# Random-feature attention and a feed-forward layer on one core: the exact fp32 projections done per head on 64 rows of the array

## The chip, the core and the metric

The kernel runs on one core of one Trainium2 chip. The metric is the device time of one execution in microseconds (us), taken as the median of several runs.

The core has five engines with queues of their own that run in order: TensorE (PE, matmuls into PSUM), VectorE (DVE), ScalarE (ACT), GpSimd (POOL) and SyncE (SP, which issues nearly all DMAs). They wait for each other by semaphores. PSUM has eight banks of 128 partitions x 512 fp32 values.

## The reference

```python
def _attn_ref(q, k, v, omega):              # q, k, v: (8, 8, 576, 64) fp32; omega: (128, 64)
    scale = 1.0 / np.sqrt(np.sqrt(D))
    q_s, k_s = (q * scale, k * scale)
    def phi(x):
        proj = np.einsum('bhsd,md->bhsm', x, omega)
        h = proj - np.sum(x * x, axis=-1, keepdims=True) / 2.0
        h = h - np.max(h, axis=-1, keepdims=True)
        return np.exp(h) / np.sqrt(m)
    q_p, k_p = (phi(q_s), phi(k_s))
    kv = np.einsum('bhsm,bhsd->bhmd', k_p, v)
    z = np.sum(k_p, axis=2)
    num = np.einsum('bhsm,bhmd->bhsd', q_p, kv)
    den = np.einsum('bhsm,bhm->bhs', q_p, z)[..., None] + 1e-06
    return num / den

def _moe_ref(x, w_in, w_out):               # x: (4608, 512) from the heads; w_in 512x2048, w_out 2048x512
    h = x @ w_in
    g = h - np.tanh(h)
    return g @ w_out
```

The term with the sum of squares is the same for all features of a token and falls out against the row maximum, so the kernel computes exp(proj - max proj) alone.

## The kernel before

Heads are taken two at a time: a pair `c` (four of them) has 128 rows of `qT` or `kT`, 64 of one head and 64 of the other, and tokens along the free dimension. A *k unit* (`k_unit(b, c)`) makes the features of the 576 keys of one batch and pair and sums them with the values into `pk`. A *q unit* (`q_unit(ch, c)`) makes the features of 256 queries (a chunk `ch`), divides them by the denominator (`L351`, `L354`, `L358`, `L360`), transposes them (`L367`) and multiplies with the k sums (`L375`). Both are generators: `tick` advances every one that is open by one piece, so that pieces of several units stand in turns in the program. A scheduler then places each engine's instructions, and the order on each engine is fixed when the program is built.

Two arithmetics are in use. The *native* one (fp32 matmuls) serves the k units of batches 0 and 1 and the q units of chunks 0, 1 and 2: 8 k units and 12 q units, all in the first stage of the program. The rest split fp32 values in two parts and use a faster format. This text is about the native ones, in `features_f`. There the stationary operand of a matmul is a block of 128 tokens of `f` (all 128 rows, both heads), and the moving one is `om_bd`, 128 rows x 256 columns: the scaled omega of head 0 in rows 0 to 63 and columns 0 to 127, that of head 1 in the other corner, and zeros elsewhere (`L105` to `L108`, made by POOL). One matmul so gives the features of both heads for 128 tokens, 256 columns. A call takes two token blocks: 512 columns, one PSUM bank `pj`. DVE takes the four row minima in one instruction (`L162`), and ACT makes four exponentials (`L164`). A k unit makes two such calls, and one more matmul for the last 64 tokens (`L198`, with `oms`, the scaled omega with no zeros beside it). A q unit makes one call. The `pj` banks go round among four (`pj0`, `pj1`, `po0`, `po1`), then three from step 16 on.

In the same stage the 16 blocks of weights (`raw`, 1 MB each, loaded by SP in one queue with `qf`, `kf` and `v`) are decoded: ACT `L439` and `L441`, POOL `L442`, DVE `L444`, `L445` and `L448`, ACT `L452`, DVE `L453` and `L454`. The buffer `m` of a decode exists once. The first feed-forward products (`L471`) stand at the end of that stage, and from there on the feed-forward layer runs with the other units between its pieces.

Of the kernel before, what the change touches and what calls it, by code (L numbers as in the profile page):

```python
# [8 lines left out]
F32 = mybir.dt.float32  # L9
# [22 lines left out]
def favor_attention_ffn(ctx: ExitStack, tc: tile.TileContext, qT, kT, va, vb, vt, omT, w, out):  # L32
# [11 lines left out]
    nc = tc.nc  # L44
# [4 lines left out]
    sb = ctx.enter_context(tc.tile_pool(name="sb", bufs=1))  # L49
    ps = ctx.enter_context(tc.tile_pool(name="ps", bufs=1, space=bass.MemoryType.PSUM))  # L50
# [34 lines left out]
    ident = const.tile([P, P], F32, name="ident")  # L85
    junk = const.tile([P, M], F32, name="junk")
# [7 lines left out]
    a0 = open_pool("a0")  # L94
    omf = a0.tile([P, M], F32, name="omf")
# [6 lines left out]
    nc.scalar.activation(ones, ident, AF.Copy, bias=1.0, scale=0.0)  # L102
    om2 = om.rearrange("p a m -> p (a m)")

    om_bd = a0.tile([P, 2, M], F32, name="om_bd")  # L105
    nc.gpsimd.memset(om_bd, 0.0)
    nc.gpsimd.tensor_scalar(om_bd[0:D, 0], omf[0:D], -SCALE, 1.0, op0=ALU.mult, op1=ALU.mult)
    nc.gpsimd.tensor_scalar(om_bd[D:P, 1], omf[D:P], -SCALE, 1.0, op0=ALU.mult, op1=ALU.mult)  # L108

    oms = a0.tile([P, M], F32, name="oms")  # L110
    nc.gpsimd.tensor_scalar(oms, omf, -SCALE, 1.0, op0=ALU.mult, op1=ALU.mult)

    def kv_tiles(pool, names):

# [17 lines left out]
    def features(lhs, name):  # L132

        n = len(lhs)
        ph = att("phi", [P, 4, M], F32, f"phi_{name}")
        nb = sb.tile([P, 4], F32, tag="nb", name=f"nb_{name}", bufs=12)

        for g in range(0, n, 2):
            m = min(2, n - g)
            pj = ps.tile([P, 2, 2 * M], F32, tag=bank("pj"), name=f"pj_{name}_{g}")  # L140
            for i in range(m):
                nc.tensor.matmul(pj[:, i], lhs[g + i], om2, start=True, stop=True)  # L142
            nc.scalar.copy(ph[:, g : g + m], pj[:, :m, M:])  # L143
            for i in range(m):
                j = g + i
                nc.vector.tensor_tensor_reduce(  # L146
                    ph[:, j], pj[:, i, :M], ph[:, j], scale=-SCALE, scalar=3.0e38,
                    op0=ALU.add, op1=ALU.min, accum_out=nb[:, j : j + 1])
        for j in range(n):
            nc.scalar.activation(ph[:, j], ph[:, j], AF.Exp, bias=nb[:, j : j + 1], scale=-1.0)  # L150
        return ph

    def features_f(f, toks, name):

        n = 2 * len(toks)
        ph = att("phi", [P, 4, M], F32, f"phi_{name}")
        nb = sb.tile([P, 4], F32, tag="nb", name=f"nb_{name}", bufs=12)
        pj = ps.tile([P, 4, M], F32, tag=bank("pj"), name=f"pj_{name}")
        for i, (a, b) in enumerate(toks):
            nc.tensor.matmul(pj[:, 2 * i : 2 * i + 2].rearrange("p a m -> p (a m)"), f[:, a:b],  # L160
                             om_bd.rearrange("p a m -> p (a m)"), start=True, stop=True)
        nc.vector.tensor_reduce(nb[:, :n], pj[:, :n], axis=AX.X, op=ALU.min)  # L162
        for j in range(n):
            nc.scalar.activation(ph[:, j], pj[:, j], AF.Exp, bias=nb[:, j : j + 1], scale=-1.0)  # L164
        return ph

    kvf = {}
    kvs = {}

    def k_unit(b, c):  # L170

        n = f"{b}_{c}"
        if not mode["native"]:
            f = att("kf", [P, S], F32, f"kf_{n}")
# [3 lines left out]
        f = att("kf", [P, 4 * P], F32, f"kf_{n}")  # L178
# [1 line left out]
        if (b, c) == (0, 0):  # L180
            fetch(0)
        v, kd = bank("v"), bank("kd")
        halves = [slice(0, D), slice(D, P)]
# [4 lines left out]
        for h, r in enumerate(halves):  # L188
            load(v[r, 4 + h, 0:D], vb[b, c, r])
        yield  # L190
        phs = []
        for t in range(0, 4, 2):
            phs.append(features_f(f, [(t * P, t * P + P), (t * P + P, t * P + 2 * P)], f"k{t}_{n}"))
            yield
        ph = att("ph5", [P, M], F32, f"ph5_{n}")
        nb = sb.tile([P, 4], F32, tag="nb", name=f"nb5_{n}", bufs=12)
        pj = ps.tile([P, M], F32, tag=bank("pj"), name=f"pj5_{n}")
        nc.tensor.matmul(pj, kd, oms, start=True, stop=True)  # L198
        nc.vector.tensor_reduce(nb[:, 0:1], pj, axis=AX.X, op=ALU.min)
# [2 lines left out]
        pk = ps.tile([P, 512], F32, tag=bank("pk"), name=f"pk_{n}")  # L202
        nc.tensor.matmul(pk[:, 0 : 2 * E], ph, v[:, 4:6].rearrange("p h e -> p (h e)"),
                         start=True, stop=False)
        for h in range(2):
            for t in range(4):
                nc.tensor.matmul(pk[:, E * h : E * h + E], phs[t // 2][:, 2 * (t % 2) + h],
                                 v[:, 6 * h + t], start=False, stop=(h, t) == (1, 3))
            if h == 0:
                yield  # L210
# [109 lines left out]
    def q_unit(ch, c):  # L320

        n = f"{ch}_{c}"
        t0 = ch * TC
        pieces = []
        t = t0
        while t < t0 + TC:
            e = min((t // S + 1) * S, t0 + TC)
            pieces.append((t // S, t - t0, e - t0))
            t = e
        f = att("qf", [P, TC], F32, f"qf_{n}")  # L330
# [1 line left out]
        load(f, qT[c, :, t0 : t0 + TC])  # L332
        yield
        if native:
            ph = features_f(f, [(0, P), (P, 2 * P)], f"q{n}")
            ix = lambda h, t: 2 * t + h
        else:
            x = att("qx", [P, 2, TC], F32R, f"qx_{n}")
            split_rows(x, f)
            yield  # L340
            ph = features([x[:, h, t * P : (t + 1) * P] for h in range(2) for t in range(2)], f"q{n}")
            ix = lambda h, t: 2 * h + t
        dn = sb.tile([P, 4], F32, tag="dn", name=f"dn_{n}", bufs=8)
# [24 lines left out]
        if native:
            qf = att("qt", [P, 2, TC], F32, f"qt_{n}")
            nc.scalar.copy(qf.rearrange("p h t -> p (h t)"), pt)  # L370
# [144 lines left out]
    def tick(new=(), force=False):  # L515
# [13 lines left out]
        pt=["pt", "h1"], h=["h0", "h1"])  # L529
# [5 lines left out]
    start = {}  # L535
# [54 lines left out]
    start = {}  # L590
# [76 lines left out]
```

## Time and profile before

| what | value |
|---|---|
| median of 3 runs | 1079.37 us (1078.85 to 1082.38) |
| profiled execution | 1079.19 us, its span 1077.4 us |
| PE busy over the span | 1048.9 us (97%) |
| DVE, ACT, POOL busy | 851.9 us (79%), 714.4 us (66%), 317.1 us (29%) |
| L160, the native projections: PE records | 64 for the k units, 48 for the q units |

The span is the time from the first to the last instruction of the profiled execution; the metric counts 1.8 us more around it. The chain of work that ended last lies on PE nearly throughout, in the feed-forward products. One fp32 matmul of the program shows as two records on PE and as two weight loads (PEld). In a timeline row the first number is the start, the second the time from the start to the end of the instructions of the row, and `x8` their number; a bracket gives the idle time ahead of it on its engine and what ended it.

### The profile page before, as it was taken

What the parts mean: (1) busy time and instruction counts of PE and PEld (TensorE: products, weight loads), DVE (VectorE), ACT (ScalarE), POOL (GpSimd) and SP (SyncE); (2) the same over time, 40 slices, a digit from 0 to 9 for tenths busy, and PEclk for the clock granted to TensorE, in tenths of its full rate; (3) what the DMA queues carried; (4) which work ended last, traced back from release to release, by engine and by line L of the source; (5) the groups of instructions that cost most, each with busy time, mean ns of one, the idle gap of its engine ahead of it and who ended that gap; (6) DMA issues with size and microseconds to landing.
All of it is one profiled execution on the core that took longest, in us unless ns stands there. A gap on an engine that the chain in (4) does not pass through costs nothing. (4 is left out here: it accounts for less than half of the span.)

```text
span 1077.4 us, 20348 instructions
## 1 busy us (share of the span) xinstructions
PE 1048.9 (97%) x6760; PEld 954.1 (89%) x6760; DVE 851.9 (79%) x3028; ACT 714.4 (66%) x1833; POOL 317.1 (29%) x526
## 2 busy tenths in 40 slices
PE   6889999998999999999999999999999999999998
PEld 5777788997999999999999998999999999999997
DVE  6899695798898886688888888898888887666522
ACT  5898564767777675677776766777767775556422
POOL 6333350344433330033333333233333331000000
PEclk8899999998999999999999999999999999999999
DMA  7653300211111110011111111021111110000000
GB/s 249 175 192 130 149 1 17 71 33 52 33 52 33 43 43 20 21 52 33 42 38 33 53 33 50 15 62 33 42 32 48 34 41 11 30 11 26 1 21 20
DMA packets 37194, 55.91 MB, mean 52 GB/s; under 512 B 13921, under 2 KB 23265, under 8 KB 35041
## 3 DMA queue, kind: packets, MB, share of 16 engines
q1 hardware_dynamic: 37008, 54.57, 16.1%
q8 instruction: 54, 0.88, 0.3%
q14 instruction: 52, 0.42, 0.1%
q10 hardware_dynamic: 80, 0.03, 0.0%
HBM read 45.15 MB, written 9.44 MB: 51 GB/s over the span
## 5 line engine op out<-in xcount | busy, mean ns | idle before, releaser
L471 PE MATMUL h<-xh,w 128*128 128x256 f32 (+1 forms) x2176 | 454.0, 292 | 3.1 <-DVE g L476 2.7
L471 PEld LDWEIGHTS h<-xh,w 128*128 128x128 f32 x2176 | 357.0, 191 | 13.3 <-DVE g L476 3.4
L471 PE MATMUL h<-xl,w 128*128 128x256 f32 (+1 forms) x1088 | 317.0, 291 | 0.5 <-DVE xl L411 0.5
L489 PE MATMUL po<-w,gh 128*128 128x512 f32 x544 | 214.3, 394 | 0.0
L471 PEld LDWEIGHTS h<-xl,w 128*128 128x128 f32 x1088 | 207.9, 191 | 6.7 <-DVE xl L411 0.8
L490 PE MATMUL po<-w,gh 128*128 128x512 f32 x544 | 213.7, 393 | 0.0
L491 PE MATMUL po<-w,gl 128*128 128x512 f32 x544 | 209.9, 391 | 0.0
L476 DVE TENSOR_TENSOR g<-h,g 128x512 f32<-128x512 f32 x144 | 98.9, 687 | 65.8 <-ACT g L475 64.9
L475 ACT ACTIVATE g<-h 128x512 f32<-128x512 f32 x144 | 85.2, 591 | 97.8 <-PE h L471 91.2
L477 ACT CAST gh<-g 128x512 fp32r<-128x512 f32 x144 | 89.4, 621 | 88.3 <-DVE g L476 85.3
L478 DVE TENSOR_TENSOR gl<-g,gh 128x512 fp32r<-128x512 f32 x144 | 111.2, 772 | 43.2 <-ACT gh L477 35.9
L491 PEld LDWEIGHTS po<-w,gl 128*128 128x128 f32 x544 | 102.2, 188 | 20.6
L489 PEld LDWEIGHTS po<-w,gh 128*128 128x128 f32 x544 | 102.6, 189 | 16.6 <-ACT gh L477 0.2
L490 PEld LDWEIGHTS po<-w,gh 128*128 128x128 f32 x544 | 102.5, 188 | 15.1
L351 DVE CUSTOM_DVE_ANT_0 junk<-phi_q,zb 128x128 f32<-128x128 f32 (+1 forms) x320 | 96.5, 304 | 15.0 <-ACT phi_q L150 0.8
L442 POOL TENSOR_SCALAR a<-a 128x1024 f32<-128x1024 f32 x16 | 63.7, 3986 | 88.0 <-ACT a L439 85.1
L254 POOL TENSOR_TENSOR khl<-phi_ka,khl 128x256 fp32r<-128x256 f32 x48 | 37.6, 785 | 159.7 <-DVE khl L253 142.3
L150 ACT ACTIVATE phi_q<-phi_q,nb_q 128x128 f32<-128x128 f32 x240 | 79.1, 392 | 4.7 <-DVE nb_q L146 4.3
L262 POOL CAST vhl<-v 128x128 fp32r<-128x128 f32 (+1 forms) x144 | 45.2, 315 | 99.5 <-PE pk L270 80.2
L391 DVE TENSOR_TENSOR ql<-pt,qh 128x512 fp32r<-128x512 f32 x60 | 41.1, 685 | 26.5 <-ACT qh L390 26.2
L146 DVE CUSTOM_DVE_ANT_0 phi_q<-pj_q,phi_q 128x128 f32<-128x128 f32 x240 | 55.8, 284 | 2.8 <-ACT phi_q L143 2.5
L263 DVE TENSOR_TENSOR vhl<-v,vhl 128x128 fp32r<-128x128 f32 (+1 forms) x144 | 44.3, 308 | 16.9 <-POOL vhl L262 13.2
(148 smaller groups left out, 1949.8 us busy)
## 6 DMA issues: line engine op xcount, KB each, us to landing
raw<-w SPq DMA_DIRECT2D x16, 1024.0 KB, 6.3
qf<-qT SPq DMA_DIRECT2D x72, 128.0 KB, 2.1
out<-o SPq DMA_DIRECT2D x36, 256.0 KB, 2.0
kf<-kT SPq DMA_DIRECT2D x24, 288.0 KB, 2.9
v<-vt SPq DMA_DIRECT2D x24, 288.0 KB, 2.9
kf<-kT SPq DMA_DIRECT2D x8, 256.0 KB, 4.1
v<-va SPq DMA_DIRECT2D x16, 128.0 KB, 3.4
kd<-kT SPq DMA_DIRECT2D x16, 16.0 KB, 4.1
```

What stands on the lines that cost most here:

```text
L146: nc.vector.tensor_tensor_reduce(ph[:, j], pj[:, i, :M], ph[:, j], scale=-SCALE, scalar=3.0e38, op0=ALU.add, op1=ALU.min, accum_out=nb[:, ...
L150: nc.scalar.activation(ph[:, j], ph[:, j], AF.Exp, bias=nb[:, j : j + 1], scale=-1.0)
L351: nc.vector.tensor_tensor_reduce(bank("junk")[r], ph[r, i], kvs[b, c][1][r, h], scale=1.0, scalar=EPS, op0=ALU.mult, op1=ALU.add, accum_ou ...
L442: nc.gpsimd.tensor_scalar(a.bitcast(F32), a.bitcast(F32), 2.0**-15, 122879.9921875, op0=ALU.max, op1=ALU.min)
L471: nc.tensor.matmul(o, w_, x, start=i == 0, stop=i == len(prods) - 1)
L475: nc.scalar.activation(g, p, AF.Tanh)
L476: nc.vector.tensor_sub(g, p, g)
L477: nc.scalar.copy(gh, g)
L478: nc.vector.tensor_sub(gl, g, gh.bitcast(F32))
L489: nc.tensor.matmul(po[t], h, wt[f][:, 0, DM:], start=first, stop=False)
L490: nc.tensor.matmul(po[t], h, wt[f][:, 1, DM:], start=False, stop=False)
L491: nc.tensor.matmul(po[t], l, wt[f][:, 0, DM:], start=False, stop=last)
```

## The change

Each head of a pair is now projected by itself. The moving operand is `oms`, 64 rows x 128 columns, and the stationary one is the 64 rows of that head; the built program puts each matmul on one half of the array's rows (rows 0 to 63, or 64 to 127). The two heads are written in turns and go to two different banks, `pjs[0]` and `pjs[1]`. `om_bd` is gone. A k unit makes one call for its four token blocks: eight matmuls of 128 columns in place of four of 256, two minima of 512 columns and eight exponentials as before, on two banks as before. A q unit makes four matmuls of 128 columns in place of two of 256, and it now uses two banks and two minima of 256 columns, in place of one bank and one of 512. The columns of `phi` and of `dn` stand head by head.

```diff
-    om_bd = a0.tile([P, 2, M], F32, name="om_bd")
-    nc.gpsimd.memset(om_bd, 0.0)
-    nc.gpsimd.tensor_scalar(om_bd[0:D, 0], omf[0:D], -SCALE, 1.0, op0=ALU.mult, op1=ALU.mult)
-    nc.gpsimd.tensor_scalar(om_bd[D:P, 1], omf[D:P], -SCALE, 1.0, op0=ALU.mult, op1=ALU.mult)
-
     oms = a0.tile([P, M], F32, name="oms")
     nc.gpsimd.tensor_scalar(oms, omf, -SCALE, 1.0, op0=ALU.mult, op1=ALU.mult)
+
+    halves = [slice(0, D), slice(D, P)]
...
-    def features_f(f, toks, name):
-
-        n = 2 * len(toks)
-        ph = att("phi", [P, 4, M], F32, f"phi_{name}")
-        nb = sb.tile([P, 4], F32, tag="nb", name=f"nb_{name}", bufs=12)
-        pj = ps.tile([P, 4, M], F32, tag=bank("pj"), name=f"pj_{name}")
-        for i, (a, b) in enumerate(toks):
-            nc.tensor.matmul(pj[:, 2 * i : 2 * i + 2].rearrange("p a m -> p (a m)"), f[:, a:b],
-                             om_bd.rearrange("p a m -> p (a m)"), start=True, stop=True)
-        nc.vector.tensor_reduce(nb[:, :n], pj[:, :n], axis=AX.X, op=ALU.min)
-        for j in range(n):
-            nc.scalar.activation(ph[:, j], pj[:, j], AF.Exp, bias=nb[:, j : j + 1], scale=-1.0)
-        return ph
+    def features_f(f, n, name):
+
+
+        if n == 2:
+            ph = att("phi", [P, 4, M], F32, f"phi_{name}")
+            phs = [ph[:, 0:2], ph[:, 2:4]]
+        else:
+            phs = [att("phi", [P, 4, M], F32, f"phi_{name}_{h}") for h in range(2)]
+        nb = sb.tile([P, 8], F32, tag="nb", name=f"nb_{name}", bufs=12)
+        pjs = [ps.tile([P, 4, M], F32, tag=bank("pj"), name=f"pj_{name}_{h}") for h in range(2)]
+        for t in range(n):
+            for h, r in enumerate(halves):
+                nc.tensor.matmul(pjs[h][:, t], f[r, t * P : (t + 1) * P], oms[r], start=True, stop=True)
+        for h in range(2):
+            b = nb[:, 4 * h : 4 * h + n]
+            nc.vector.tensor_reduce(b, pjs[h][:, :n], axis=AX.X, op=ALU.min)
+            for t in range(n):
+                nc.scalar.activation(phs[h][:, t], pjs[h][:, t], AF.Exp, bias=b[:, t : t + 1], scale=-1.0)
+        return phs
...
-        phs = []
-        for t in range(0, 4, 2):
-            phs.append(features_f(f, [(t * P, t * P + P), (t * P + P, t * P + 2 * P)], f"k{t}_{n}"))
-            yield
+        phs = features_f(f, 4, f"k{n}")
+        yield
+        yield
...
-                nc.tensor.matmul(pk[:, E * h : E * h + E], phs[t // 2][:, 2 * (t % 2) + h],
+                nc.tensor.matmul(pk[:, E * h : E * h + E], phs[h][:, t],
                                  v[:, 6 * h + t], start=False, stop=(h, t) == (1, 3))
...
-            ph = features_f(f, [(0, P), (P, 2 * P)], f"q{n}")
-            ix = lambda h, t: 2 * t + h
+            ph = features_f(f, 2, f"q{n}")
+            at = lambda h, t: ph[h][:, t]
```

The scheduler places the instructions of the first stage anew. On every engine the order is the same, row for row, from the last native q unit on (on PE from its products `pn_3`, `L375`, at 113.68 us in the profile); SP's order is the same throughout. Three places of the first stage are shown. Lines of the changed kernel stand one lower than before from `L198` on, and `L162`, `L165` and `L167` are now the projections, the minima and the exponentials.

**PE**, from the end of the second k unit over the third k unit and the first q unit to the sums `pk` of the second (the names of k units end in batch, pair and buffer number before, and in pair, head and buffer number now; pairs count from 0). Before:

```order
L160 MATMUL pj_k_0_1_218<-om_bd,kf_1_186 128x256 x2
L198 MATMUL pj_0_1_258<-oms,kd_126 128x128
L225 MATMUL pk_0_210<-ident,z_0_252 128x128 x2
L160 MATMUL pj_k_0_2_264<-om_bd,kf_2_226 128x256 x2
L160 MATMUL pj_k_0_2_286<-om_bd,kf_2_226 128x256 x2
L160 MATMUL pj_q_0_296<-om_bd,qf_0_272 128x256 x2
L203 MATMUL pk_1_278<-v_123,ph_0_1_256 128x132
L207 MATMUL pk_1_278<-v_123,phi_k_0_1_200 128x66 x2
```

Now:

```order
L162 MATMUL pj_k_1_0_202<-oms,kf_1_185 128x128
L162 MATMUL pj_k_1_1_203<-oms,kf_1_185 128x128
L199 MATMUL pj_0_1_260<-oms,kd_122 128x128
L226 MATMUL pk_0_222<-ident,z_0_254 128x128 x2
L162 MATMUL pj_k_2_0_267<-oms,kf_2_228 128x128 x4
L162 MATMUL pj_k_2_1_268<-oms,kf_2_228 128x128 x4
L162 MATMUL pj_q_0_0_301<-oms,qf_0_287 128x128 x2
L204 MATMUL pk_1_293<-v_119,ph_0_1_258 128x132
L208 MATMUL pk_1_293<-v_119,phi_k_1_0_199 128x66 x4
L162 MATMUL pj_q_0_1_302<-oms,qf_0_287 128x128 x2
L208 MATMUL pk_1_293<-v_119,phi_k_1_1_200 128x66 x4
```

The alternation of the heads as written stands in PE's queue for the first two k units alone (the first two rows end the second of them). From the third on, the four blocks of head 0 stand together, and then the four of head 1. The projection of a q unit is in two pieces, and here the second of them stands behind half of the sums `pk`.

**ACT**, from its first exponentials on (`a` and `m` are the buffers of a decode, `w` its result). Before:

```order
L164 ACTIVATE phi_k_0_0_152<-pj_k_0_0_154,nb_k_0_0_153 128x128 x4
L439 ACTIVATE a_162<-raw_142 128x1024
L441 ACTIVATE m_163<-raw_142 128x1024
L164 ACTIVATE phi_k_0_0_176<-pj_k_0_0_178,nb_k_0_0_177 128x128 x4
L200 ACTIVATE ph_0_0_194<-pj_0_0_196,nb_0_0_195 128x128
L439 ACTIVATE a_234<-raw_150 128x1024
L452 CAST w_170<-a_162 128x1024
L222 COPY kvf_106<-pk_0_210 128x64 x2
L441 ACTIVATE m_235<-raw_150 128x1024
L439 ACTIVATE a_357<-raw_174 128x1024
```

Now:

```order
L440 ACTIVATE a_171<-raw_138 128x1024
L442 ACTIVATE m_172<-raw_138 128x1024
L167 ACTIVATE phi_k_0_0_148<-pj_k_0_0_151,nb_k_0_150 128x128 x4
L167 ACTIVATE phi_k_0_1_149<-pj_k_0_1_152,nb_k_0_150 128x128 x4
L201 ACTIVATE ph_0_0_193<-pj_0_0_195,nb_0_0_194 128x128
L440 ACTIVATE a_236<-raw_146 128x1024
L453 CAST w_179<-a_171 128x1024
L223 COPY kvf_102<-pk_0_222 128x64 x2
L442 ACTIVATE m_237<-raw_146 128x1024
L440 ACTIVATE a_379<-raw_183 128x1024
```

The first two instructions of the first decode have moved ahead of the first eight exponentials.

**DVE**, around the minima of the third k unit and of the first q unit. Before:

```order
L162 TENSOR_REDUCE nb_k_0_2_285<-pj_k_0_2_286 128x4
L454 SCALAR_TENSOR_TENSOR w_242<-m_235,a_234 128x1024
L444 TENSOR_SCALAR a_357<-a_357 128x1024
L162 TENSOR_REDUCE nb_q_0_295<-pj_q_0_296 128x4
L445 SCALAR_TENSOR_TENSOR a_357<-raw_174,a_357 128x1024
L214 COPY z_1_326<-pk_1_278 128x2
L448 SCALAR_TENSOR_TENSOR m_358<-raw_174,m_358 128x1024
L199 TENSOR_REDUCE nb_0_2_331<-pj_0_2_332 128x1
L162 TENSOR_REDUCE nb_k_0_3_344<-pj_k_0_3_345 128x4
L351 ISA junk,dn_0_304<-phi_q_0_294,zb_0_276 128x128
```

Now:

```order
L445 TENSOR_SCALAR a_379<-a_379 128x1024
L446 SCALAR_TENSOR_TENSOR a_379<-raw_183,a_379 128x1024
L165 TENSOR_REDUCE nb_k_2_266<-pj_k_2_1_268 128x4
L165 TENSOR_REDUCE nb_q_0_300<-pj_q_0_0_301 128x2
L449 SCALAR_TENSOR_TENSOR m_380<-raw_183,m_380 128x1024
L352 ISA junk,dn_0_313<-phi_q_0_299,zb_0_291 128x128
L352 ISA dn_0_313 128x1
L352 ISA junk_101,dn_0_313<-phi_q_0_299,zb_0_291 128x128
L352 ISA dn_0_313 128x1
L165 TENSOR_REDUCE nb_q_0_300<-pj_q_0_1_302 128x2
```

`z_1`, which waits for the sums `pk` of the second k unit, stood right behind this piece of the third decode; it has moved further down, behind the denominators (`L352`, shown as ISA) and the end of that decode. The minima of the q unit are two, with other work between them.

More of the change, by code (lines that the diff above doesn't have):

```diff
@@ L151, in features @@
         return ph
-    def features_f(f, toks, name):
-        n = 2 * len(toks)
-        ph = att("phi", [P, 4, M], F32, f"phi_{name}")
-        nb = sb.tile([P, 4], F32, tag="nb", name=f"nb_{name}", bufs=12)
-        pj = ps.tile([P, 4, M], F32, tag=bank("pj"), name=f"pj_{name}")
-        for i, (a, b) in enumerate(toks):
-            nc.tensor.matmul(pj[:, 2 * i : 2 * i + 2].rearrange("p a m -> p (a m)"), f[:, a:b],
-                             om_bd.rearrange("p a m -> p (a m)"), start=True, stop=True)
-        nc.vector.tensor_reduce(nb[:, :n], pj[:, :n], axis=AX.X, op=ALU.min)
-        for j in range(n):
-            nc.scalar.activation(ph[:, j], pj[:, j], AF.Exp, bias=nb[:, j : j + 1], scale=-1.0)
-        return ph
+    def features_f(f, n, name):
[4 more added lines that the diff above has]
+            phs = [att("phi", [P, 4, M], F32, f"phi_{name}_{h}") for h in range(2)]
+        nb = sb.tile([P, 8], F32, tag="nb", name=f"nb_{name}", bufs=12)
+        pjs = [ps.tile([P, 4, M], F32, tag=bank("pj"), name=f"pj_{name}_{h}") for h in range(2)]
[8 more added lines that the diff above has]
+        return phs
     kvf = {}
@@ L182, in k_unit @@
         v, kd = bank("v"), bank("kd")
-        halves = [slice(0, D), slice(D, P)]
         for r in halves:
@@ L190, in k_unit @@
         yield
-        phs = []
-        for t in range(0, 4, 2):
-            phs.append(features_f(f, [(t * P, t * P + P), (t * P + P, t * P + 2 * P)], f"k{t}_{n}"))
-            yield
+        phs = features_f(f, 4, f"k{n}")
+        yield
+        yield
         ph = att("ph5", [P, M], F32, f"ph5_{n}")
-        nb = sb.tile([P, 4], F32, tag="nb", name=f"nb5_{n}", bufs=12)
+        nb = sb.tile([P, 8], F32, tag="nb", name=f"nb5_{n}", bufs=12)
         pj = ps.tile([P, M], F32, tag=bank("pj"), name=f"pj5_{n}")
@@ L341, in q_unit @@
             ph = features([x[:, h, t * P : (t + 1) * P] for h in range(2) for t in range(2)], f"q{n}")
-            ix = lambda h, t: 2 * h + t
+            at = lambda h, t: ph[:, 2 * h + t]
         dn = sb.tile([P, 4], F32, tag="dn", name=f"dn_{n}", bufs=8)
@@ L345, in q_unit @@
             for t in range(2):
-                i = ix(h, t)
+                i = 2 * h + t
                 for b, s, e in pieces:
@@ L351, in q_unit @@
                         nc.vector.tensor_tensor_reduce(
-                            bank("junk")[r], ph[r, i], kvs[b, c][1][r, h], scale=1.0, scalar=EPS,
+                            bank("junk")[r], at(h, t)[r], kvs[b, c][1][r, h], scale=1.0, scalar=EPS,
                             op0=ALU.mult, op1=ALU.add, accum_out=dn[r, i : i + 1])
@@ L355, in q_unit @@
         for i in range(4):
-            e = bank("norm")
+            e, x = bank("norm"), at(i // 2, i % 2)
             if e is nc.scalar:
-                e.mul(ph[:, i], ph[:, i], dn[:, i : i + 1])
+                e.mul(x, x, dn[:, i : i + 1])
             else:
-                e.tensor_scalar(ph[:, i], ph[:, i], dn[:, i : i + 1], 1.0, op0=ALU.mult, op1=ALU.mult)
+                e.tensor_scalar(x, x, dn[:, i : i + 1], 1.0, op0=ALU.mult, op1=ALU.mult)
         yield
@@ L366, in q_unit @@
         for i in range(4):
-            nc.tensor.transpose(pt[:, i * P : (i + 1) * P], ph[:, ix(i // 2, i % 2)], ident)
+            nc.tensor.transpose(pt[:, i * P : (i + 1) * P], at(i // 2, i % 2), ident)
         if native:
```

## The prediction

> **What bounds the kernel now.** First the page's busy times, then the windows view, which splits the span into stretches (busy time and number of records of PE, PEld, DVE, ACT and POOL, then the granted clock, the DMA share and GB/s).
>
> ```profile
> PE 1048.9 (97%) x6760; PEld 954.1 (89%) x6760; DVE 851.9 (79%) x3028; ACT 714.4 (66%) x1833; POOL 317.1 (29%) x526
> ...
> 0.00:20.00 20.00, 14.74 (x53) 12.82 (x54) 9.25 (x13) 8.61 (x18) 12.55 (x32) 0.76 0.77 246
> 20.00:40.00 20.00, 15.48 (x75) 13.46 (x73) 17.03 (x33) 15.51 (x42) 8.28 (x2) 0.81 0.69 203
> 40.00:110.00 70.00, 59.98 (x340) 50.35 (x341) 68.92 (x216) 63.20 (x172) 23.42 (x6) 1.00 0.45 159
> ...
> 114.00:200.00 86.00, 85.70 (x421) 72.47 (x420) 60.28 (x112) 49.36 (x81) 27.19 (x13) 1.00 0.18 66
> ```
>
> PE is the bound over the whole span, but not where the change is. From 40 to 110 us DVE is busy 68.9 of 70 us, while PE has 10.0 us idle; from 114 us PE has 0.3 us idle in 86. So the native stage is DVE's until about 110 us, and what comes behind it is PE's. Where the two meet is read from the timeline:
>
> ```profile
> 97.42 0.50 PE L471 MATMUL h<-xh,w 128*128 128x512 f32 x1 [1.60 <-DVE g L476]
> 109.55 0.50 PE L471 MATMUL h<-xh,w 128*128 128x512 f32 x1 [0.78 <-DVE g L476]
> ...
> 113.68 1.36 PE L375 MATMUL pn<-qt,kvf 128*128 128x64 f32 x8 [0.68 <-ACT qt L370]
> ```
>
> Twice the feed-forward products wait for a DVE subtraction that stands in DVE's full queue; from 113.68 us on the order of all engines is unchanged. My reading is therefore that the change counts by what it does to DVE's queue up to about 110 us, and that a shift there goes through to the end one for one. What PE gains or loses in projections counts only beyond its 10.0 us of idle time.
>
> **The projections on PE.** Starts in a row without idle time give what one matmul costs:
>
> ```profile
> 70.01 1.03 PE L160 MATMUL pj_q<-om_bd,qf 128*128 128x256 f32 x4
> 70.88 0.38 PE L225 MATMUL pk<-ident,z 128*128 128x128 f32 x2
> 71.09 1.03 PE L160 MATMUL pj_q<-om_bd,qf 128*128 128x256 f32 x4
> ...
> L160 PE MATMUL pj_k<-om_bd,kf x64: 379/380/766, 5.1 to 78.5; 128*128 128x256 f32 x64
> L160 PE MATMUL pj_q<-om_bd,qf x48: 377/379/483, 26.6 to 89.4; 128*128 128x256 f32 x48
> ```
>
> Four records, two matmuls of 256 columns, take 0.87 us from start to start, so one takes 0.435 us; one of 128 columns takes 0.21 us. Before there are 112 records, 56 matmuls: 24.4 us. Now there are 112 matmuls of 128 columns. If a matmul on 64 rows takes what one on 128 rows takes, and none runs beside another, that is 112 x 0.21 = 23.5 us. If all ran in pairs it would be 11.8 us, a gain of up to 12.6 us of PE time. But two can run beside each other only where the heads alternate, and in the new order they do so in the first two k units alone; elsewhere the blocks of one head stand together, and a q unit's two pieces are often apart. I take no gain on the path (bounds: 12.6 us less work, and none); either way it falls into PE's idle time between 40 and 110 us. Before 40 us the gain is that of the first two units, 16 matmuls in 8 pairs, 8 x 0.21 = 1.7 us, and twice that at the low clock of that stretch; DVE is then in the first decodes, so I leave it out of the sum and keep it for the low end.
>
> **DVE.** The one added work is the split minimum of the 12 q units:
>
> ```profile
> 23.18 0.68 DVE L162 TENSOR_REDUCE nb_k<-pj_k 128x4 f32<-128x512 f32 x1
> 23.78 0.28 DVE L199 TENSOR_REDUCE nb<-pj 128x1 f32<-128x128 f32 x1
> 23.98 0.68 DVE L162 TENSOR_REDUCE nb_k<-pj_k 128x4 f32<-128x512 f32 x1
> ```
>
> From start to start 512 columns take 0.60 us and 128 take 0.20. On the line between them 256 take 0.33, and two of these 0.67: 0.07 us more for each, 12 x 0.07 = **+0.8 us**. By durations (0.68 and 0.28, so 0.41 for 256) it would be 12 x 0.14 = 1.7 us. I take the starts, since a full queue pays those. All of it lies in the stretch where DVE is the bound, and nothing hides it. The minima of the k units, all exponentials and all else on ACT keep their number and size. The two POOL instructions and the memset for `om_bd` go; the projections then wait for `kf`, as they nearly do now, so nothing comes of that.
>
> **The first decode moves ahead.**
>
> ```profile
> 1.98 0.42 SPq L80 DMA_DIRECT2D raw<-w  x1
> ...
> DMA to landing us min/median/max: 5.7/5.7/5.7
> ...
> 7.93 1.14 ACT L164 ACTIVATE phi_k<-pj_k,nb_k 128x128 f32<-128x128 f32 x4 [4.99 <-DVE nb_k L162]
> 8.95 1.13 ACT L439 ACTIVATE a<-raw 128x1024 f32<-128x1024 f32 x1
> ...
> 10.23 7.21 POOL L442 TENSOR_SCALAR a<-a 128x1024 f32<-128x1024 f32 x2 [3.79 <-ACT a L439]
> ...
> 13.89 1.52 DVE L444 TENSOR_SCALAR a<-a 128x1024 uint32<-128x1024 uint32 x1 [1.54 <-POOL a L442]
> ```
>
> The first weights land at 1.98 + 5.7 = 7.7 us. ACT's step on them stood behind four exponentials, at 8.95; it now leads ACT's queue. DVE waits for the end of this chain at 13.89, and it comes 8.95 - 7.7 = **-1.2 us** sooner. What pays is the first exponentials: they start 2.0 us later (two steps of about 1.0 us from start to start). The ninth of them, on which the sums `pk` wait, comes at the same time as before, since ACT does the same 11 instructions up to it, back to back.
>
> **The wait for `z` goes, and the load behind `qf` is late.**
>
> ```profile
> DVE z L214 <- PE pk L207: 1.8, 1, 1.8
> DVE nb_k L162 <- PE pj_k L160: 1.0, 2, 0.7
> ...
> 26.58 1.10 PE L160 MATMUL pj_q<-om_bd,qf 128*128 128x256 f32 x4 [2.35 <-DMA qf<-qT]
> 27.52 0.50 PE L203 MATMUL pk<-v,ph 128*128 128x132 f32 x2
> 27.81 3.52 PE L207 MATMUL pk<-v,phi_k 128*128 128x66 f32 x16
> ...
> 31.37 0.16 DVE L214 COPY z<-pk 128x2 f32<-128x2 f32 x1 [1.83 <-PE pk L207]
> ...
> 26.63 1.41 SPq L80 DMA_DIRECT2D qf<-qT x2
> 28.09 0.44 SPq L80 DMA_DIRECT2D raw<-w  x1
> ...
> raw<-w SPq DMA_DIRECT2D x16, 1024.0 KB, 6.3
> ...
> 42.10 1.18 ACT L439 ACTIVATE a<-raw 128x1024 f32<-128x1024 f32 x1
> ```
>
> Before, DVE stands still for 1.83 us until `z` of the second pair. In the new order four denominators and the end of a decode stand ahead of that `z`: **-1.8 us**. But the second piece of the q projection now stands behind half of the `pk` records (3.52 / 2 = 1.8 us) and the first one (0.3 us), and only then is `qf` read to its end. SP's third `qf` waits for that buffer, and a load of weights is next in SP's queue. So that load goes out about 2.1 us later, at 30.2 in place of 28.09, and with the page's 6.3 us lands at 36.5. ACT took it at 42.10 before, but in the new order it stands ahead of the exponentials of the fourth k unit, some 6 us earlier, and these and a decode's `w` queue behind it, for which DVE waits in turn. I cannot tell from the trace how much of this wait falls open: between 0 and 2.1 us. I take **+1.6**, near the upper end, because ACT has 20 - 15.5 = 4.5 us idle between 20 and 40 us and so comes to it early.
>
> **The sum.** +0.8 - 1.2 - 1.8 + 1.6 = -0.6 us on the profiled execution's 1079.19 us, which is 0.18 under the median: **1078.6 us**.
>
> **The rivals.** (1) The lead is kept: the late load costs nothing, and the two waits of DVE for the projections (1.0 us in the row above) go too, as PE has fewer rows ahead of them. 1079.19 + 0.8 - 1.2 - 1.8 - 1.0 = **1076.0**; with the 1.7 us of the paired units at most 1074.3. For it speaks that DVE's queue has other work there, against it that it moves whatever stalls to the next decode.
>
> (2) The banks. The native stage uses 8 x 3 + 12 x 1 = 36 banks before and 8 x 3 + 12 x 2 = 48 now, from the same four, later three. PE already waits for them:
>
> ```profile
> PE pj_k L160 <- ACT phi_q L164: 1.8, 1, 1.8
> PE pj_q L160 <- ACT phi_q L164: 1.4, 1, 1.4
> PE pj_k L160 <- ACT phi_k L164: 1.1, 1, 1.1
> ```
>
> These 4.3 us (from 40 to 114 us) become 4.3 x 48 / 36 = 5.7 by their number, and 8.6 if the shorter lead doubles them; half of the added 1.4 to 4.3 us reaching DVE, +0.7 to +2.2 on the sum: up to **1080.8**. Against it: a q unit's bank is now held for two exponentials, not four.
>
> (3) Slower: changing between 64 and 128 rows costs PE time. The new order has 30 runs of projections with other matmuls between them. The fifth k unit's projections started here:
>
> ```profile
> 40.22 2.17 PE L160 MATMUL pj_k<-om_bd,kf 128*128 128x256 f32 x8 [1.09 <-ACT phi_k L164]
> ```
>
> Of the 30 runs 22 stand from that unit on, so behind 40 us; each is one change in and one out, 44 in all. No row before shows such a change. The nearest row is a record's tail: 380 ns of duration against 217 from start to start, 0.163 us. 44 x 0.163 = 7.2 us, still within 10.0 us of idle time; it decides from 10.0 / 44 = 0.23 us a change on. At twice the tail it is 44 x 0.33 = 14.4, 4.4 over: 1079.19 + 4.4 = **1083.6**. The other bound is a change that costs nothing, which is my forecast. The Trainium skill, "TensorEngine Tiling (Array Packing)", Tiling Modes, Key Properties, states that going from one tiling mode to another drains TensorE. It gives no time for it, and no run here shows it, since every matmul before uses all 128 rows; with one tail for each drain the sum stays as it is, and with two it is this rival.
>
> (4) The change does not do what it says: with the heads grouped in the queue, or with no overlap between row halves at all, PE's work is the same 23.5 us. That gives the forecast's time, as the sum has no gain from it.
>
> **How the numbers follow.** About 0.3% (3.2 us) is what a measurement of this kernel can tell from no change: 1076.1 and 1082.6 are the limits. Forecast, with (4): 0.45. (1): 0.20, with more than half of it under 1076.1. (2): 0.17, nearly all within. (3): 0.18, nearly all above 1082.6. So faster 0.13, same 0.69, slower 0.18. The likeliest case alone reaches from 1077 to 1080.5; the range takes in most of (1) and (3): 1075 to 1084.
>
> **What would show it.** Right: 256-column minima near 0.33 us from start to start; the first decode step on ACT near 7.7 us and the first DVE step of the decode near 12.7; no wait for `z` near 31 us, but one for `a` or `w` between 34 and 40; the first products `pn_3` of the last native q unit within 2 us of 113.68, and the same time from there to the end. Rival (3) shows as gaps on PE ahead of and behind each run of projections, and PE without idle time from 40 to 110 us. Wrong would be a first stage shorter by 4 us or more, which would mean that the projections on PE were on the path, or an end that moves by more than `pn_3` does.

## The result, and the profile after

| kernel | median, us | range, us | runs |
|---|---|---|---|
| before | 1079.97 | 1078.85 to 1082.38 | 4 |
| changed | 1094.24 | 1093.62 to 1095.23 | 4 |

The ratio is 1.0126, interval 1.0109 to 1.0144: the change makes the kernel 14 us slower. The profiled execution took 1095.23 us, its span is 1093.5 us, 16.1 us longer than before. (Executions in which the chip was disturbed are left out of all comparisons, and a profile that fell into one was taken anew.)

The page's busy times and row of the granted clock, and then the windows view in the stretches that matter (busy time and records of PE, PEld, DVE, ACT and POOL, the granted clock, DMA share, GB/s), all of the changed kernel:

```profile
PE 1071.0 (98%) x6872; PEld 971.8 (89%) x6872; DVE 852.8 (78%) x3040; ACT 716.5 (66%) x1833; POOL 317.6 (29%) x523
...
PEclk7659899998999999999999999999999999999999
...
20.00:40.00 20.00, 17.48 (x92) 15.65 (x90) 18.13 (x36) 16.43 (x43) 12.29 (x3) 0.66 0.63 188
40.00:46.00 6.00, 3.69 (x22) 2.83 (x23) 5.96 (x19) 4.17 (x10) 0.57 (x1) 1.00 0.38 102
46.00:77.00 31.00, 31.00 (x116) 24.89 (x117) 16.42 (x61) 17.55 (x57) 3.66 (x1) 0.52 0.31 90
77.00:110.00 33.00, 32.23 (x214) 26.42 (x214) 31.63 (x102) 29.13 (x78) 11.89 (x3) 0.99 0.68 242
```

DVE has the same total work as before, PE 22 us more busy time with only 112 records more. The third number from the end says where that comes from. From 46 to 77 us PE runs at half clock (0.52 with the edges), has no idle time, and DVE, which was the bound of this stage, is busy for 16.42 us of 31. Before, the clock was 1.00 from 40 us on. The same stretch of the kernel before, and the longest wait of PE in it:

```profile
46.00:77.00 31.00, 25.15 (x147) 20.78 (x145) 30.59 (x94) 29.25 (x88) 8.85 (x3) 1.00 0.50 159
...
65.95 1.13 PE L160 MATMUL pj_k<-om_bd,kf 128*128 128x256 f32 x4 [1.76 <-ACT phi_q L164]
```

The timeline of the changed kernel shows how the stretch begins, what a row costs in it, and where the stage ends; the row of 111.64 begins a second, shorter low stretch (0.66 in the window from 110 to 120 us):

```profile
43.01 1.16 PE L162 MATMUL pj_k<-oms,kf 64*128 64x128 f32 x8 [0.48 <-ACT phi_q L167]
46.00 0.30 PE L368 MATMUL pt<-ident,phi_q 128*128 128x128 f32 x1 [1.83 <-DVE phi_q L361]
...
61.10 2.07 PE L162 MATMUL pj_k<-oms,kf 64*128 64x128 f32 x8
63.11 0.69 PE L226 MATMUL pk<-ident,z 128*128 128x128 f32 x2
...
111.64 0.75 PE L368 MATMUL pt<-ident,phi_q 128*128 128x128 f32 x4 [1.59 <-DVE phi_q L361]
...
130.67 1.26 PE L376 MATMUL pn<-qt,kvf 128*128 128x64 f32 x8
```

The same eight half-row records (`64*128`) take 1.16 us at 43.01 and 2.07 us at 61.10. The last native products stand at 130.67 us in place of 113.68, 17.0 us later, and the span is 16.1 us longer. Waits of PE of 1.4 to 1.8 us stood in the kernel before too (1.45 us ahead of 53.30, 1.76 ahead of 65.95), and its clock stayed at 1.00. Why it falls here and stays down is the question of the experiments.

### The profile page after: what moved, and what is told of

It is laid out like the page before. It is cut to its first block, busy times and chain, and to the rows that moved or that the text cites. A ratio compares the mean times of both kernels' runs of the same rounds, so it can differ in the third digit from the quotient of the medians.

```text
span 1093.5 us, 20598 instructions
## 1 busy us (share of the span) xinstructions
PE 1071.0 (98%) x6872; PEld 971.8 (89%) x6872; DVE 852.8 (78%) x3040; ACT 716.5 (66%) x1833; POOL 317.6 (29%) x523
## 5 line engine op out<-in xcount | busy, mean ns | idle before, releaser
L352 DVE CUSTOM_DVE_ANT_0 junk<-phi_q,zb 128x128 f32<-128x128 f32 (+1 forms) x320 | 94.7, 299 | 15.7 <-ACT phi_q L167 0.8
```

The lines of the kernel that those rows point to most:

```text
L352: nc.vector.tensor_tensor_reduce(bank("junk")[r], at(h, t)[r], kvs[b, c][1][r, h], scale=1.0, scalar=EPS, op0=ALU.mult, op1=ALU.add, accum ...
```

## The experiments

"Order pinned" means that every instruction of the first stage keeps the changed kernel's place on its engine, so that two kernels differ only in what is named. Theory A of the first expectations, that half rows hold the clock down, took this form after the first three runs: **half-row matmuls keep a high clock but do not raise a low one**.

**e1: all 128 rows, everything else as changed.** The order is pinned on PE, DVE and ACT; the banks, the split minima and the two heads' separate matmuls stay:

```diff
-                nc.tensor.matmul(pjs[h][:, t], f[r, t * P : (t + 1) * P], oms[r], start=True, stop=True)
+                nc.tensor.matmul(pjs[h][:, t], f[:, t * P : (t + 1) * P], om_bd[:, h], start=True, stop=True)
```

`om_bd[:, h]` has zeros in the rows of the other head.

> The changed kernel with the order of PE, DVE, ACT and SP kept row for row, but each projection uses all 128 rows: the stationary operand is the token block of both heads, the moving one 128 columns with zeros in the other head's rows. Theory A (matmuls on half of the rows keep the granted clock at one half from 50 to 77 us): the clock is 1.00 from about 40 us on and the time is 1078 to 1084 us. Theory B (the new order lets PE idle at 44 to 46 us, and the clock falls through that, whatever the rows): clock 0.50 from 50 to 77 us again, 1090 to 1096 us. Theory C (going from 128 to 64 rows and back costs about 0.18 us for each run of projections, 30 runs, 5.4 us, and the clock is a side effect): about 1088 us.

Measured: 1080.64 us, ratio to before 1.0005 (0.999 to 1.002). The whole loss is gone with the 64 rows; the new order, the second bank and the split minima together cost nothing that can be measured. The same kernel again, for its trace:

> The same kernel as in e1: the changed kernel's order on every engine, row for row, but each native projection on all 128 rows with a zero-padded weight of its head. Wanted here is its trace. Theory A (half-row matmuls do not raise a low clock): the granted clock is 1.00 from about 40 us to the end of the native stage although PE waits as in the changed kernel (1.83 us before the transposes at 46.00), pn_3 starts at 113 to 115 us, time 1079 to 1082 us. Rival B (PE's wait at 44 to 46 us lowers the clock whatever runs behind it): the windows from 46 to 77 us show 0.50 here too, and then the time must have been got back elsewhere.

1079.58 us. Its windows and PE's timeline at the places shown of the changed kernel:

```profile
46.00:77.00 31.00, 28.41 (x222) 26.36 (x221) 28.98 (x108) 29.33 (x91) 8.52 (x3) 1.00 0.62 190
...
45.16 0.30 PE L430 MATMUL pt<-ident,phi_q 128*128 128x128 f32 x1 [1.68 <-DVE phi_q L423]
45.39 1.16 PE L224 MATMUL pj_k<-om_bd,kf 128*128 128x128 f32 x8
46.38 0.38 PE L288 MATMUL pk<-ident,z 128*128 128x128 f32 x2
46.60 0.49 PE L430 MATMUL pt<-ident,phi_q 128*128 128x128 f32 x3
...
114.24 1.26 PE L438 MATMUL pn<-qt,kvf 128*128 128x64 f32 x8
```

The wait is there (1.68 us), and the clock is 1.00 behind it. `pn_3` is 0.6 us later than before. Rival B, the wait alone, falls; e1's ratio says that this is not one lucky execution.

**e4: the heads truly in turns.** PE's order is the changed kernel's but for one thing: in every native projection the two heads' matmuls alternate, at the place of the second head. The scheduler sets the other engines' order.

> The changed kernel with PE's order set so that the two heads of every native projection stand in turns in PE's queue, at the place where the second head's part stood; DVE and ACT are placed anew for it. Each pair can then run side by side, so PE's projections take about half of the time (12 us less at full clock), in 20 runs in place of 30. Theory A, if the clock goes by the rows that are busy at a time: it stays at 1.00 from about 40 us on, and the time is 1076 to 1082 us; if it goes by each matmul's own rows, it is low again and the time is 1084 to 1090 us. Theory B: low clock after the first idle of PE, 1086 to 1096 us. Theory C: 20 x 0.18 = 3.6 us in place of 5.4, so 1.8 us less than the changed kernel, about 1092 us.

Measured: 1090.24 us (1087.04 to 1094.39), ratio 1.0101 (1.0064 to 1.0138). Its windows:

```profile
40.00:46.00 6.00, 6.00 (x29) 4.82 (x30) 5.30 (x17) 4.43 (x14) 1.00 (x1) 0.50 0.07 22
46.00:77.00 31.00, 26.87 (x187) 22.03 (x185) 23.18 (x91) 22.64 (x68) 4.71 (x2) 0.82 0.50 147
...
73.51 1.16 PE L187 MATMUL pj_k<-oms,kf 64*128 64x128 f32 x16
```

Running side by side does shorten the projections: sixteen records take 1.16 us here at full clock, as long as eight take in e1b at 45.39. But the low clock is there, earlier (0.50 in windows of 2 us from 24 to 46 us, and again from 52 to 60), and DVE again has idle time. The time alone does not tell theory A from B: it lies in B's range and at the upper edge of A's second one.

**e5: streams of one kind.** A kernel that computes nothing of the reference: fp32 matmuls back to back, each stream behind a wait of about 5 us for DVE unless said. In short (`N` is 80; single groups of four matmuls between and behind the streams are left out):

```python
half(w, N, 0)                      # 64 rows; directly behind a stream on all rows
w = gap(1); half(w, N, 0)          # 64 rows behind a wait
w = gap(2); turns(w, 2 * N)        # the two row halves in turns
w = gap(3)
for _ in range(N // 8):
    half(w, 4, 0); full(w, 4)      # four on 64 rows, four on 128
w = gap(4); narrow(w, N)           # 128 rows, 66 columns
w = gap(5)
for _ in range(N // 16):               # 64 rows and 66 columns in turns
    half(w, 4, 0); narrow(w, 4); half(w, 4, 1); narrow(w, 4)
```

> Computes nothing of the reference: streams of native fp32 matmuls on PE alone, with waits of about 7 us for DVE between them. In order: 80 on all rows, then at once 80 on rows 0 to 63; wait; 80 on rows 0 to 63; wait; 160 in turns on rows 0 to 63 and 64 to 127, two banks; wait; runs of four on half and four on all rows; wait; 80 on all rows with 66 columns; wait; runs of four on half rows and four of 66 columns. Theory A: the clock goes to 1.00 within some 4 us in the stream on all rows, falls to 0.50 in the stream on half rows and never leaves 0.50 when half rows start cold; runs in turns at 1.00 if it goes by rows busy at a time. Theory B: every stream without idle time is at 1.00 after some 4 us. Theory C: runs of four and four take about 0.2 us more per pair of runs than 8 x 0.21 us.

PE's timeline (a start, a duration, the form with its rows, the records) and then the windows over the same streams, in which the clock is the third number from the end:

```profile
7.37 20.19 PE L37 MATMUL bank<-w,f 128*128 128x128 f32 x160 [7.37 <-DVE w L64]
30.22 18.68 PE L47 MATMUL bank<-w,f 64*128 64x128 f32 x168
53.99 35.52 PE L47 MATMUL bank<-w,f 64*128 64x128 f32 x168 [5.09 <-DVE w L64]
96.28 20.12 PE L52 MATMUL bank<-w,f 64*128 64x128 f32 x320 [4.76 <-DVE w L64]
171.15 34.40 PE L41 MATMUL bank<-w,f 128*128 128x66 f32 x160 [4.76 <-DVE w L64]
...
8.00:12.00 4.00, 4.00 (x22) 4.00 (x22) 0.00 (x0) 0.00 (x0) 1.00 0.00 0
12.00:27.00 15.00, 15.00 (x137) 15.00 (x136) 0.00 (x0) 0.00 (x0) 1.00 0.00 1
30.00:48.00 18.00, 18.00 (x164) 17.88 (x164) 0.00 (x0) 0.00 (x0) 1.00 0.01 2
60.00:89.00 29.00, 29.00 (x141) 29.00 (x141) 0.29 (x1) 0.00 (x0) 0.50 0.00 1
100.00:116.00 16.00, 16.00 (x286) 16.00 (x284) 0.00 (x0) 0.00 (x0) 0.99 0.01 2
140.00:165.00 25.00, 25.00 (x101) 22.08 (x101) 0.58 (x2) 0.00 (x0) 0.50 0.00 1
180.00:205.00 25.00, 25.00 (x119) 25.00 (x118) 0.00 (x0) 0.00 (x0) 0.50 0.00 1
```

The first stream, on all rows and behind a wait of 7.37 us, is the control: 22 records from 8 to 12 us are the pace of half clock (0.18 us each), 137 from 12 to 27 us that of full clock (0.11). The column of the clock shows 1.00 for both, so this rise is read from the pace alone. Half rows right behind all-row matmuls keep 1.00 for the whole 18.7 us, with PE at 0.111 us a record, where theory A had expected a fall. The same stream behind a wait stays at 0.50 for 35.5 us, though PE never idles. The row halves in turns reach full clock after 4 us (the window of 96 to 100 us has 0.50) and give 320 records in 20.1 us, two at a time. The mix of four and four, and all rows with 66 columns, stay at 0.50 to their end, and so do half rows and 66 columns in turns of four (213 to 252 us). The native stage is made of just these: half rows, 66-column sums and short pieces of all rows between them. The Trainium skill, "TensorE: Matmul & The Clock Gate", Part 1, states that some 3.4 us of sustained activity release the clock; the stream in turns agrees (0.50 for 4 us, then 0.99), that on half rows does not (0.50 for 35.5 us), and the measurement decides.

**e6: a bridge over the wait.** The changed kernel, order pinned, and eight all-row matmuls more at the place of the 1.83 us wait; the transposes then write over what they leave. Nothing is taken away. The edit in short, without its place in the pinned order:

```diff
         pt = ps.tile([P, 2 * TC], F32, tag=bank("pt"), name=f"pt_{n}")
+        for _ in range(8 if (ch, c) == (1, 0) else 0):
+            nc.tensor.matmul(pt[:, 0:P], ident, ident, start=True, stop=True)
```

> The changed kernel with its order pinned on every engine, and eight 128x128 all-row matmuls of ident more (about 0.22 us each, 1.75 us) into the transposes' own PSUM tile, in the place where PE waits 1.83 us for phi_q (44.2 to 46.0 us); the transposes write over them. PE does more work, nothing is removed. Theory A (the clock falls at that wait and half-row matmuls keep it down): the clock stays 1.00 from 37 us to 110 us, most of the 14 us come back: 1079 to 1085 us. Rival (the price of the runs themselves, about 0.18 us each at full clock, fills PE whatever the clock): 1092 to 1096 us, as the changed kernel. Rival (the clock falls a little later, at the next short wait): 1086 to 1094 us.

Measured: 1087.4 us median, ratio 1.0045 (1.0023 to 1.0068). Its ten executions fall in two groups: four from 1079.85 to 1081.88 us and six from 1087.24 to 1090.38. The profile is of one of the first group, 1081.88 us:

```profile
44.55 2.05 PE L157 MATMUL pt<-ident 128*128 128x128 f32 x16
46.64 1.16 PE L230 MATMUL pj_k<-oms,kf 64*128 64x128 f32 x8
47.72 0.43 PE L296 MATMUL pk<-ident,z 128*128 128x128 f32 x2
47.99 0.49 PE L439 MATMUL pt<-ident,phi_q 128*128 128x128 f32 x3
...
46.00:77.00 31.00, 29.88 (x207) 24.48 (x206) 28.17 (x101) 28.40 (x91) 7.38 (x2) 1.00 0.56 172
...
116.59 1.26 PE L447 MATMUL pn<-qt,kvf 128*128 128x64 f32 x8
```

With the wait filled the clock is 1.00 from 40 to 100 us, DVE is busy for 28.17 of 31 us in place of 16.42 (PE, at 29.88, has little idle time left), and `pn_3` comes 14.1 us earlier than in the changed kernel, 2.9 us later than before. More work on PE made the kernel faster. The slower group has no trace; its mean clock, 0.974 to 0.976 against 0.979 to 0.986, says that something lowered it in those executions too, but not where.

**e9: a kick in the low stretch.** The wait stays; 14 all-row matmuls stand in one piece in the middle of the half-clock stretch, in the `pk` tile of the fourth k unit. The edit in short, as for e6:

```diff
         pk = ps.tile([P, 512], F32, tag=bank("pk"), name=f"pk_{n}")
+        for _ in range(14 if (b, c) == (0, 3) else 0):
+            nc.tensor.matmul(pk[:, 0:P], ident, ident, start=True, stop=True)
```

> The changed kernel, order pinned on every engine, with 14 all-row 128x128 matmuls of ident in one piece into the pk group's own PSUM tile, right ahead of that group at 49.83 us, that is in the middle of the stretch in which PE runs at 0.50 and waits for nothing. PE is given 14 x 0.22 us = 3.1 us more work at full clock, up to 6 us at half. Theory A (it is the low clock that half rows do not raise, and a dense piece of all-row work does): the clock goes to 1.00 at the end of that piece, at 54 to 56 us and not at 77, and stays; of the 15 us lost in 46 to 77 us at half clock some 11 are not lost, against some 5 us of added work: 1084 to 1091 us, faster than the changed kernel although PE has more to do. Rival (PE is simply overfull): 1096 to 1100 us.

Measured: 1088.12 us (1086.69 to 1089.03), 6.1 us faster than the changed kernel; ratio to before 1.0063 (1.0048 to 1.0078).

```profile
46.87 0.30 PE L439 MATMUL pt<-ident,phi_q 128*128 128x128 f32 x1 [1.83 <-DVE phi_q L431]
47.10 2.04 PE L230 MATMUL pj_k<-oms,kf 64*128 64x128 f32 x8
...
51.48 4.57 PE L157 MATMUL pk<-ident 128*128 128x128 f32 x28
55.89 0.39 PE L274 MATMUL pk<-v,ph 128*128 128x132 f32 x2
```

The eight records at 47.10 take 2.04 us, at half clock. Then 28 records of all rows take 4.4 us, and behind them the two `pk` records start 0.23 us before the next row, at full clock. In windows of 2 us the clock is 0.50 from 48 to 54 us and 1.00 from 54 to 104. So the clock comes back some 2.5 us into a dense piece on all rows, and half rows then keep it for 50 us. This is the run that shows cause and effect most plainly: the stretch that ended at 77 us now ends at 54. (A second fall follows here too, as in the changed kernel: 0.50 from 106 to 112 us.)

**e10 and e11: half rows on one side of the wait only.** Order pinned; ahead of the wait at 44 us all rows and behind it 64 (e10), and the reverse (e11, with `not early`). `EARLY` holds the seven units ahead of the wait; of the eighth, `k1_0`, only the first head stands ahead of it.

```diff
+                early = name in EARLY or (name, h) == ("k1_0", 0)
+                if early:
+                    nc.tensor.matmul(pjs[h][:, t], f[:, t * P : (t + 1) * P], om_bd[:, h], start=True, stop=True)
+                else:
+                    nc.tensor.matmul(pjs[h][:, t], f[r, t * P : (t + 1) * P], oms[r], start=True, stop=True)
```

> The changed kernel's order pinned on every engine. The native projections ahead of PE's wait at 44 to 46 us (all up to the first head of the fifth k unit) take all 128 rows with a zero-padded weight, those behind it 64 rows as in the changed kernel. If the half rows ahead of a wait decide whether it lowers the clock: the clock is 1.00 behind the wait, later waits may lower it: 1080 to 1088 us. If the half rows behind it decide (they do not keep the clock over a wait): 0.50 from 47 us to about 77 us as in the changed kernel: 1091 to 1096 us.

> The mirror of e10: 64 rows up to that wait, all 128 rows behind it. If the half rows ahead of a wait decide whether the clock falls: it falls at about 47 us, and rises again within some 6 us since all-row matmuls raise it: 1081 to 1085 us. If those behind decide: no fall at 47 us: 1079 to 1082 us. In both a long stretch at 0.50 like that of 46 to 77 us would speak against theory A.

e10: its executions took 1080.21, 1094.06, 1095.88 and 1109.00 us, too far apart for the ratio (1.0172, 1.0089 to 1.0255) to be clear. The profile is of the first; there the clock held over the 1.68 us wait, and the half rows kept it:

```profile
45.49 0.30 PE L436 MATMUL pt<-ident,phi_q 128*128 128x128 f32 x1 [1.68 <-DVE phi_q L429]
45.72 1.16 PE L230 MATMUL pj_k<-oms,kf 64*128 64x128 f32 x8
...
46.00:77.00 31.00, 29.83 (x205) 24.28 (x204) 28.22 (x105) 28.43 (x89) 7.38 (x2) 1.00 0.58 178
```

So the same program, with the same wait and half rows behind it, takes 1080 or 1095 us. That the clock fell in the longer executions is read only from their mean clocks (0.973, 0.970 and 0.958 against 0.987). e11: 1082.61 us, ratio 1.0023 (1.0006 to 1.0041), all ten executions below 1085.6:

```profile
20.00:40.00 20.00, 17.80 (x82) 16.10 (x82) 17.56 (x35) 15.96 (x41) 12.22 (x3) 0.50 0.63 188
40.00:46.00 6.00, 6.00 (x21) 4.60 (x21) 5.93 (x18) 4.15 (x11) 0.90 (x1) 0.50 0.08 22
46.00:77.00 31.00, 28.59 (x198) 26.41 (x198) 26.07 (x95) 26.03 (x83) 7.39 (x2) 0.89 0.55 159
...
49.74 1.92 PE L228 MATMUL pj_k<-om_bd,kf 128*128 128x128 f32 x8
```

Both forecasts took the clock to be high ahead of 47 us. Here it never rose before: 0.50 from 10 to 52 us. From 40 to 52 us PE was never idle, with half rows and 66-column sums for the most part, and that did not raise it; 3 us after the first projection on all rows, at 49.74, it is 1.00, and it stays so to the end of the stage. It costs little, because up to 46 us DVE is as busy as before (17.56 of 20 and 5.93 of 6 us): the low clock is dear only where it makes PE the bound.

**e2 and e3: one part of the change alone** (k units by heads with q units as before, and the reverse; the scheduler sets the order).

> One part of the change alone: the k units' projections by heads on 64 rows, the q units' as before on 128 rows with the block-diagonal weight; the scheduler sets the order. Theory A: fewer half rows (6 k units of 8 matmuls in place of these and 12 q units of 4) leave more all-row work between them, so the clock falls less or later: 1080 to 1090 us. If a change of rows had a price that alone decides (0.09 us per run, 12 of 36 runs): 1080 to 1084 us. If the 256-column minimum decides: 1079 to 1081 us.

> The other part alone: the q units' projections by heads on 64 rows, the k units' as before. Theory A: half-row work is spread through 30 to 115 us in short runs; the clock falls where PE waits between such runs: 1080 to 1092 us. If only the k units matter (their runs of 4 matmuls are the longest): 1079 to 1081 us.

e2: 1082.92 us, ratio 1.0016 (1.0000 to 1.0032). e3: 1089.29 us, 1.0072 (1.0053 to 1.0092). The q units' part costs more, and the two do not add up to 1.0126. In e3's trace the clock falls four times between 40 and 108 us (to 0.50 near 42, 58, 68 and 106); in e2's twice (near 56 and 68). The expectations overlapped so far that these runs tell only which part is dearer.

**e7 and e8: can the early low clock be lifted with profit?** e7 is e6 with matmuls of `ident` in four more waits; e8 is the kernel before with 16 and 6 of them in two waits.

> As e6, with matmuls of ident in four more of PE's waits: 7 before the kd projection at 8.26 us, 15 before the pk group at 12.13 us, 11 before the second half of the third k unit at 23.23 us, 7 before the transposes at 111.64 us. Theory A: the clock is 1.00 in nearly all of the native stage, also from 10 to 37 us where it was 0.51 to 0.66; that part is not bound by PE alone, so 1 to 3 us below e6: 1077 to 1083 us. Rival (price of the runs): 1092 to 1097 us. Rival (filler delays what it stands before): 1 to 3 us above e6.

> The kernel before, its order pinned, with 16 matmuls of ident in PE's wait before the pk group at 12.47 us and 6 in the wait before the second half of the third k unit at 23.10 us. Theory A: the clock from 10 to 38 us (0.53, 0.84, 0.78 in the kernel before) comes nearer to 1.00; but PE waits for DVE and ACT there, so the time stays: 1077 to 1081 us. Rival (a low clock costs on the path there too): 1072 to 1076 us.

e7: 1085.74 us, 1.0056 (1.0024 to 1.0088). Its clock is 1.00 from 10 to 20 us, against 0.51 in the changed kernel, and nothing comes of it. e8: 1080.9 us, 1.0010 (0.9998 to 1.0023), with the clock at 0.88 and 0.95 in the first two 20 us against 0.76 and 0.81. Neither beats the kernel before; no version did. But e8's trace shows something of use here. On all rows, too, the clock falls behind waits of PE, at about 63 us (1.31 us) and at about 97 us (1.60 us):

```profile
63.01 2.06 PE L228 MATMUL pj_k<-om_bd,kf 128*128 128x256 f32 x4 [1.31 <-ACT phi_q L232]
```

In windows of 2 us the clock is 0.76, 0.50 and 0.88 from 62 to 68 us and 0.80, 0.50 and 0.85 from 96 to 102, and 1.00 around them: some 3.4 us of low clock each time, where the changed kernel has 31.

## Why the prediction was wrong

The prediction said 1078.6 us and "same" with 0.69; the time is 1094.24, outside its range.

- **What bounds the kernel, and that a shift of `pn_3` goes through one for one**: right for the kernel before; in the changed one PE takes DVE's place as the bound from 46 to 77 us. `pn_3` moved by 17.0 us and the profiled time by 16.0.
- **The terms of the sum on DVE and ACT**: right, and close in size. The rows of the changed kernel, in order of time:

```profile
7.56 1.12 ACT L440 ACTIVATE a<-raw 128x1024 f32<-128x1024 f32 x1 [4.63 <-DMA raw<-w]
12.49 0.69 DVE L445 TENSOR_SCALAR a<-a 128x1024 uint32<-128x1024 uint32 x1 [1.53 <-POOL a L443]
27.16 0.41 DVE L165 TENSOR_REDUCE nb_q<-pj_q 128x2 f32<-128x256 f32 x1
27.49 1.21 DVE L449 SCALAR_TENSOR_TENSOR m<-raw,m 128x1024 uint32<-128x1024 uint32 x1
32.65 0.15 DVE L215 COPY z<-pk 128x2 f32<-128x2 f32 x1
35.55 1.19 ACT L440 ACTIVATE a<-raw 128x1024 f32<-128x1024 f32 x1 [0.57 <-DMA raw<-w]
38.99 0.69 DVE L454 TENSOR_SCALAR a<-a 128x1024 uint32<-128x1024 uint32 x1 [1.14 <-ACT w L453]
```

  The first decode starts at 7.56 and reaches DVE at 12.49 (7.7 and 12.7 were forecast); a minimum of 256 columns takes 0.33 us from start to start; `z` waits for nothing; the late load is seen on ACT (0.57 us) and DVE waits 1.14 us behind it (1.6 was taken). e1b has the same terms with the old rows (DVE in the first decode at 12.33, `z` at 32.23 without a wait), but only 0.40 us of the wait behind the load; the ratio of e1 is 1.0005 (0.999 to 1.002), where the sum had -0.6 us.
- **The projections on PE**: this is the step that failed. It took its durations from rows at full clock, "either way it falls into PE's idle time between 40 and 110 us", and bounded this term with a gain of 12.6 us and none, with no loss. That the clock of 1.00 in the windows row of 40 to 110 us could depend on the change was never asked, although the prediction's own rows had 0.76 and 0.81 for the first 40 us. What the runs showed in its place: from 47 to 77 us the clock is 0.50, and eight half-row records take 2.01 us from start to start at 61.10, where the prediction's 0.21 us a matmul gives 0.84. The 31 us of PE's work from 46 to 77 would take some 15.5 at full clock (an estimate, half of it), which is about the size of the loss. With all 128 rows in the same order (e1) the loss is gone, and a dense all-row piece (e9) ends the low stretch.
- **Rival (3)** had the sign, and a part of what would show it (PE without idle time, but from 46 to 77 us alone), but the wrong cause and a third of the size. A change between 64 and 128 rows does cost time, now measured: eight half-row records and the two behind them take 47.99 - 46.64 = 1.35 us in e6 and 46.60 - 45.39 = 1.21 in e1b, so 0.14 us a run, 0.07 a change. Over the same instructions up to the next long wait, with the clock at 1.00 in both (46.64 to 96.60 us in e6, 45.39 to 94.14 in e1b), e6 has 48.80 us of busy PE and e1b 45.36: 3.4 us more, or 0.08 us for each of 42 changes. That is half a tail, below the 0.23 from which it decides, and it is hidden for the most part, as the forecast said: from the same starts to `pn_3` e6 takes 116.59 - 46.64 = 69.95 us and e1b 114.24 - 45.39 = 68.85, 1.1 us more, and a fall of e6's clock from 100 to 104 us lies in that too.
- **Rivals (1) and (2)**, the kept lead and the banks: e1 has the order and the banks and shows neither. **Rival (4)**, no overlap, is right where the heads stand grouped: at full clock eight half-row records take 1.16 us at 43.01, no less than eight all-row ones in e1b. But the forecast's time did not follow from it.
- What stays open: the rule by which the clock falls. Waits of 1.83 us lowered it in the changed kernel and e9, one of 1.68 us did not in e1b, and in e10 not in each execution, and in e8 it fell behind shorter ones on all rows. So half rows are not needed for a fall; what the runs show of them is that they lengthen it. e6 shows that filling the wait avoids the long stretch, not that such a wait must cause it, and why six of its ten executions are slower is not known.

## What to carry to other kernels

Before rows, columns or gaps of a matmul are changed, look at the granted clock of the stage and ask what raises it there: a stage in which PE is only 86% busy can have it at 1.00 by work that the change thins out. When PE turns up at 100% busy with few records in a window, read the clock ahead of the instruction costs; a few dense all-row matmuls put into the stretch (e9) tell in one run whether the clock is the cause. A change of array rows that saves nothing on the path puts that clock at risk without a return.

## What was not expected of the hardware

- fp32 matmuls on 64 rows held a clock of 1.00 for 18.7 us behind all-row work, and stayed at 0.50 for 35.5 us behind a wait. All rows with 66 columns (34.4 us) and a mix of four and four (44 us) stayed at 0.50 too. Two row halves in turns raised it within 4 us and ran two at a time (0.063 us a record with the slow start).
- At half clock a change of rows is dearer: in e5's mix a run of eight records takes 2.00 us where 8 x 0.211 = 1.69 would do, 0.31 us a change against 0.07 to 0.08 at full clock.
